# Attention and top-1 experts: q, k and v laid out in tiles before the launch, the bias added on VectorE

## The chip, the cores and the metric

One core of a Trainium2 chip: TensorE (PE, with its weight loads as PEld), VectorE (DVE), ScalarE (ACT), GpSimd (POOL), SyncE (SP, which issues most DMAs). The metric is the device time of one launch in microseconds. What numpy does to the arrays before the launch is not part of it.

## The reference

Attention over 8 batches, 8 heads, 576 positions and 64 features, with a causal window of 128 and a bias that falls linearly with distance; then each of the 4608 tokens goes to the one expert (of 8) with the largest cosine to it.

```python
scores = scale * np.matmul(q, k.transpose(0, 1, 3, 2))
rel = pos[:, None] - pos[None, :]
bias = slopes[:, None, None] * (-np.abs(rel).astype(np.float32))[None, :, :]
mask = (rel >= 0) & (rel < window)
scores = np.where(mask, scores + bias[None], -1000000000.0)
attn = np.exp(scores - np.max(scores, axis=-1, keepdims=True))
attn = attn / (np.sum(attn, axis=-1, keepdims=True) + 1e-09)
out = np.matmul(attn, v)
...
logits = xn @ en.T / tau              # xn, en: rows of x = attention's output and of expert_emb, normalized
expert_idx = np.argmax(logits, axis=1)
out[mask] = gate_w[mask, None] * (np.maximum(x[mask] @ w1[e], 0.0) @ w2[e])
```

## The kernel before, in words

The attention stage works on 36 tiles of 128 query rows, in the order of `tiles`: for each pair of batches, four tiles of the one (the first of kind "first", three "full"), four of the other, and a "pair" tile with the last 64 rows of both. Each tile is two units of four heads (72 units, `u`), so 16 first, 48 full and 8 pair units. A query sees its own tile's keys and the tile's before.

For each tile `load` (L413) brings q, k and v as 128 rows by 512 features, one piece of 64 floats per row and head. `prep_pe` (L492) turns q and k on TensorE (four matmuls each, against the identity, into a PSUM bank of tag "pt"), and `prep_copy` (L526 on VectorE, L528 on ScalarE) copies them to SBUF with features on the partitions, q with the factor -1/8. `on_dve` and `SHARE` deal out the copies between the two engines. A batch's keys lie in two blocks of SBUF, so that tile 2 of a batch takes its keys from both.

A unit then runs through these steps:
- `score_pe`: for each of two PSUM banks one bias matmul (L592; for a first tile the table `tab_first` against the identity, else the rank-two factors `row` and `col` that `factors` builds), then the products of q and k (L598) added onto it. The scores are negated, with the keys of the own tile and of the tile before side by side: 256 columns a head.
- `merge_dve` (L607, L610): one predicated copy takes, for each position in a window, the one of the two columns that is in it. First tiles need none.
- `max_dve` (L615): one reduction per bank, over the 128 columns of each of two heads.
- `exp_act` (L622) on ScalarE, one instruction for a head; `probs_pe` (L630) turns the probabilities on TensorE; `probs_act` (L481) and `probs_dve` (L484) write them as a high and a low half-precision part; `mask_pool` (L650, L663) on GpSimd separates what belongs to the own tile (`md`) from what belongs to the tile before (`mp`).
- `values_pe` (L682, L698): six matmuls a head, 24 a unit. In a pair tile the own part is three a head and the part before is three for each batch, whose operand has 64 rows of queries (36 a unit).
- `sums_dve` and `normalize` (L714, L720) divide by the sums.

After both units of a tile, x is split into two half-precision parts (`x_act` L734 and L736, `x_pool` L747), its norm is summed (L743), it is turned by a DMA (L751), and the logits are formed (L757, L761). Tiles are routed in groups of 8, 8, 8, 6, 4 and 2: a chain of small operations (L825 to L854) gives each token its place, and an indirect DMA from GpSimd (L863) puts its row into the expert's segment in DRAM.

Beside this the "head" runs: after the third group the expert with most tokens is picked, its weights are fetched and split (L912 on ScalarE, L916 on VectorE), and its first 384 rows are computed by TensorE (L945, L969) in whatever time is left. After the last put, the stage of the experts (`moe`) begins with L1374; it is not touched.

The order on each engine is not written by hand. `Plan` takes jobs with an engine, a duration in ns, what they follow, which buffers they make and use, and a due time (`STEP` times the unit plus `DUE` of the step); it lists them greedily, per engine the job that could start first, and among those within `SLACK` ns of it the one due first. Jobs with `fill=True` (the head's) come after all others. The queues then run in that order, each instruction waiting for its semaphores. Buffers: four PSUM banks for scores, two for turned probabilities and values (tag "ps"), two for turned q and k and small things (tag "pt").

## Time and profile before

| | |
|---|---|
| Median of three runs | 689.68 us (685.45 to 692.1) |
| The profiled execution | 690.15 us, its span 688.4 us, mean granted TensorE clock 0.971 |
| TensorE busy in the span | 643.3 us |
| VectorE, ScalarE, GpSimd busy | 377.8, 340.8, 261.4 us |

The span runs from the first to the last instruction of one execution. Rows of busy time count a stretch once however many instructions overlap in it. Instructions of one engine overlap: one that follows closely starts before the one in front has ended, so the pace of a kind is read from start to start, not from its duration. A half clock of TensorE (1.2 in place of 2.4 GHz) shows as 0.5 in the clock column.

### The profile page before, as it was taken

To read this page: it belongs to the slowest core of one execution; us is meant where nothing else is said; L and a number is where in the kernel's file an instruction comes from. 1 tells how busy PE (TensorE), PEld (TensorE's weight loads), DVE (VectorE), ACT (ScalarE), POOL (GpSimd) and SP (SyncE) were. 2 spreads that over 40 slices of the span, in tenths; PEclk is the share of its full clock that TensorE was granted. 3 is DMA by queue.
4 is the path that set the end of the run, shared out by engine and by line. 5 is a ranking of instruction groups with operands and counts; after the bars stand their busy time and mean duration, and the time that the engine had idled before them with its cause. 6 is when DMAs were issued, how large, how long until landed. Compare 5 with 4: busy or idle time off the path is not lost. (4 is left out here: it accounts for less than half of the span.)

```text
span 688.4 us, 15704 instructions
## 1 busy us (share of the span) xinstructions
PE 643.3 (93%) x6043; PEld 425.1 (62%) x6043; DVE 377.8 (55%) x974; ACT 340.8 (49%) x794; POOL 261.4 (38%) x472
## 2 busy tenths in 40 slices
PE   7999999999999988992999999999999999999993
PEld 4777767777776755641665467476584764754442
DVE  5877786776789969642335724344244255310250
ACT  5999888977887955410235523343243244210210
POOL 7667687767777837552010210120111112001011
PEclk9999999998999999886999999999999999999998
DMA  8588969886988895136999973934919545001000
GB/s 200 125 184 191 194 170 206 159 214 129 201 156 229 196 206 161 41 109 149 249 250 358 250 262 55 269 123 67 318 63 240 202 99 200 16 16 47 13 31 31
DMA packets 217676, 109.83 MB, mean 160 GB/s; under 512 B 195829, under 2 KB 195829, under 8 KB 217600
## 3 DMA queue, kind: packets, MB, share of 16 engines
q1 hardware_dynamic: 211760, 89.89, 55.7%
q0 software_dynamic: 5840, 18.92, 7.2%
q8 instruction: 48, 0.79, 0.5%
q14 instruction: 28, 0.23, 0.1%
HBM read 61.92 MB, written 28.12 MB: 131 GB/s over the span
## 5 line engine op out<-in xcount | busy, mean ns | idle before, releaser
L1374 PE MATMUL ps<-xT,w1h 128*128 128x272 f16 (+7 forms) x896 | 175.4, 296 | 13.4 <-DMA xT<-xs 12.2
L1374 PE MATMUL ps<-xT,w1l 128*128 128x272 f16 (+7 forms) x448 | 132.4, 296 | 0.0
L1374 PEld LDWEIGHTS <-w1h 128*128 128x128 f16 x896 | 88.2, 99 | 44.8 <-issue 14.1
L384 POOL DMA_INDIRECT out_dram<-y,ids x32 | 35.6, 1112 | 203.5 <-DVE y L1432 105.3
L1382 DVE SCALAR_TENSOR_TENSOR hl<-ps,hh 128x272 f16<-128x272 f32 (+7 forms) x112 | 51.7, 475 | 105.9 <-ACT hh L1384 99.5
L1384 ACT ACTIVATE hh<-ps 128x272 f16<-128x272 f32 (+7 forms) x112 | 45.6, 425 | 114.7 <-PE ps L1374 114.7
L622 ACT ACTIVATE pe<-sc,nm 128x128 f32<-128x128 f32 x288 | 87.7, 390 | 24.6 <-DVE nm L615 13.7
L1418 PE MATMUL ps<-w2h,hh 128*128 128x512 f16 (+1 forms) x264 | 98.4, 373 | 0.0
L1418 PE MATMUL ps<-w2l,hh 128*128 128x512 f16 (+1 forms) x264 | 98.4, 373 | 0.0
L1418 PE MATMUL ps<-w2h,hl 128*128 128x512 f16 (+1 forms) x264 | 98.4, 373 | 0.0
L1418 PEld LDWEIGHTS <-hh 128*128 128x128 f16 x528 | 51.5, 98 | 58.6 <-issue 0.8
L598 PE MATMUL sc<-k,q 64*128 64x128 f32 (+2 forms) x768 | 74.8, 339 | 0.5 <-ACT q L528 0.5
L484 DVE SCALAR_TENSOR_TENSOR pq<-ptp,pq 128x512 f16<-128x512 f32 x72 | 53.1, 738 | 20.3 <-ACT pq L481 18.1
L598 PEld LDWEIGHTS sc<-k,q 64*128 64x128 f32 (+1 forms) x768 | 51.0, 180 | 19.3 <-issue 16.4
L481 ACT ACTIVATE pq<-ptp 128x512 f16<-128x512 f32 x72 | 55.0, 764 | 14.4 <-PE ptp L630 8.8
L615 DVE TENSOR_REDUCE nm<-sc 128x2 f32<-128x256 f32 x144 | 58.5, 416 | 3.2 <-PE sc L598 2.9
L630 PE MATMUL ptp<-ident,pe 128*128 128x128 f32 x288 | 48.0, 287 | 8.0 <-ACT pe L622 3.6
L1349 DVE SCALAR_TENSOR_TENSOR w2l<-ws,w2h 128x1024 f16<-128x1024 f32 x28 | 33.9, 1223 | 36.2 <-ACT w2h L1351 36.0
L1374 PEld LDWEIGHTS <-w1l 128*128 128x128 f16 x448 | 44.1, 99 | 15.1 <-DVE w1l L1349 0.3
L1349 DVE SCALAR_TENSOR_TENSOR w1l<-ws,w1h 128x1024 f16<-128x1024 f32 x28 | 33.4, 1222 | 34.0 <-ACT w1h L1351 33.9
L747 POOL TENSOR_TENSOR gx<-xf,gx 128x512 f16<-128x512 f32 x36 | 42.7, 1187 | 19.7 <-ACT gx L734 8.5
L698 PE MATMUL av<-vh,mp 128*128 128x65 f16 (+1 forms) x512 | 49.0, 200 | 0.5 <-POOL mp L650 0.5
(233 smaller groups left out, 1174.1 us busy)
## 6 DMA issues: line engine op xcount, KB each, us to landing
ws<-moe_w_dram SPq DMA_DIRECT2D x56, 512.0 KB
ldk<-k_dram SPq DMA_DIRECT2D x32, 256.0 KB
ldq<-q_dram SPq DMA_DIRECT2D x32, 256.0 KB
ldv<-v_dram SPq DMA_DIRECT2D x32, 256.0 KB
stg<-moe_w_dram SPq DMA_DIRECT2D x16, 256.0 KB
xs<-zrow SPq DMA_DIRECT2D x3, 1092.2 KB
xs<-zrow SPq DMA_DIRECT2D x1, 1413.5 KB
xs<-zrow SPq DMA_DIRECT2D x1, 1285.0 KB
```

The costliest lines, as they stand in the source:

```text
L481: nc.scalar.activation(hi, ps, AF.Copy, scale=scale)
L484: nc.vector.scalar_tensor_tensor(lo, ps, scale, hi, op0=ALU.mult, op1=ALU.subtract)
L598: nc.tensor.matmul(sc[T, hf, j][o, l, w], qx[rows, hp, o], at["x"][rows, hp, kc], start=False, stop=(l == 1), skip_group_check=True)
L615: nc.vector.tensor_reduce(nm_t[T, hf][:, j, :], sc[T, hf, j][:, :, 0:P], axis=AX.X, op=ALU.min)
L622: nc.scalar.activation(pr_t[T, hf][:, 2 * l + j, :], ps[:, l, 0:P], AF.Exp, bias=nm[:, l : l + 1], scale=-1.0)
L630: nc.tensor.transpose(pt[:, i, :], pe[:, i, :], ident)
L698: nc.tensor.matmul(o_, a_, b_, start=False, stop=(n == last), skip_group_check=True)
L1349: nc.vector.scalar_tensor_tensor(lo_, x, SW, hi, op0=ALU.mult, op1=ALU.subtract)
L1374: nc.tensor.matmul(ps[:, :w], a[:, kt, fs], xx[:, b + kt, c0 : c0 + w], start=(n == 0), stop=(n == len(jobs) - 1))
L1382: nc.vector.scalar_tensor_tensor(hl[:, ft, c0 : c0 + w], ps[:, :w], 0.0, hi, op0=ALU.max, op1=ALU.subtract)
L1384: nc.scalar.activation(hi, ps[:, :w], AF.Relu)
L1418: nc.tensor.matmul(ps, x[:, ft, a * P : (a + 1) * P], w[:, ft, c], start=(n == 0), stop=(n == len(jobs) - 1))
```

## The change

Numpy now lays q out as one array per tile with 128 features (two heads) on the partitions, k as one per batch in blocks of 64 positions, also with features on the partitions, and v as one per tile with rows on the partitions. A tile's loads go straight into the operands of the score matmuls, with 2 KB in one piece for each partition, and a batch's keys lie in one SBUF tile. Turns, copies, the bias matmuls and their factors are gone; the factor 1/8 goes to the exponential. Two PSUM banks that they used become one, and turned probabilities and values get three. VectorE adds the bias from a table of 16-bit values and takes the maximum in one instruction for a head, after the merge, writing the sum back to PSUM: four in a unit in place of two reductions. For pair tiles `mask_pool` writes two operands of 128 rows, padded with zeros, so that all of their value matmuls are wide. The planner's jobs, prices, due times, step and slacks change with it. One cast of x in four goes to VectorE up to tile 26, as before, and none after (before: one in two).

```diff
-RING = {'sc':'sc','pt':'pt','ptp':'ps','av':'ps','lg':'pt','misc':'pt'}
-BANKS = {'sc':4,'ps':2,'pt':2}
+RING = {'sc':'sc','ptp':'ps','av':'ps','lg':'pt','misc':'pt'}
+BANKS = {'sc':4,'ps':3,'pt':1}
-KBUFS = {"k0": 2, "k1": 2, "q": 3}
+KBUFS = {"k": 3, "q": 4}
-STEP = 3038
-SLACK = {'PE': 100, 'ACT': 100, 'DVE': 50, 'POOL': 400, 'SP': 300}
+STEP = 2426
+SLACK = {'PE': 104, 'ACT': 98, 'DVE': 44, 'POOL': 541, 'SP': 49}
-SHARE = {'v': 0, 'x': 0.25, 'q': 0, 'k': 0, 'v2': 0, 'x2': 0.5, 'q2': 0.5, 'k2': 0.25}
+SHARE = {'v': 0, 'x': 0.25, 'v2': 0, 'x2': 0}
...
+    def bias_table(kind):
+        rel = rels[kind]
+        m = const.tile([P, P], I32, name=f"mask_{kind}")
+        wrap = const.tile([P, P], F32, tag="wrap", name=f"wrap_{kind}")
+        nc.vector.tensor_scalar(m, rel, 0.0, None, op0=ALU.is_ge)
+        nc.vector.tensor_scalar(wrap, rel, 0.0, float(WIN), op0=ALU.is_lt, op1=ALU.mult)
+        nc.vector.tensor_tensor(wrap, wrap, rel, op=ALU.add)
+        tab = const.tile([P, H, P], BF16, name=f"tab_{kind}")
+        for h in range(H):
+            nc.vector.tensor_scalar(tab[:, h, :], wrap, -slopes[h] / QS, None, op0=ALU.mult)
...
+        def load(T, nm):
+            kind, b, t = tiles[T]
+            if nm == "q":
+                qT[T] = qk.tile([P, HP, P], F32, tag="q", name=f"q_{T}", bufs=KBUFS["q"])
+                nc.sync.dma_start(qT[T], q[T].rearrange("p (a c) -> p a c", a=HP))
+            elif nm == "k":
+                for x in (b, b + 1) if kind == "pair" else (b,):
+                    if x not in kT:
+                        kT[x] = qk.tile([P, S // REM, HP, REM], F32, tag="k", name=f"k_{x}", bufs=KBUFS["k"])
+                    c = slice(P // REM * t, S // REM if kind == "pair" else P // REM * (t + 1))
+                    nc.sync.dma_start(kT[x][:, c], k[x].rearrange("p (n a c) -> p n a c", a=HP, c=REM)[:, c])
...
         def score_pe(T, hf):
...
-                nc.tensor.matmul(ps[:, :, 0 : b_.shape[-1]], a_, b_, start=True, stop=False, skip_group_check=True)
...
                         nc.tensor.matmul(
-                            sc[T, hf, j][o, l, w], qx[rows, hp, o], at["x"][rows, hp, kc], start=False, stop=(l == 1), skip_group_check=True
+                            sc[T, hf, j][o, l, w].rearrange("p (n c) -> p n c", c=REM),
+                            qT[T][rows, hp, o],
+                            kT[x][rows, kc, hp, :],
...
-        def max_dve(T, hf, j):
+        def max_dve(T, hf, j, l):
...
-            nc.vector.tensor_reduce(nm_t[T, hf][:, j, :], sc[T, hf, j][:, :, 0:P], axis=AX.X, op=ALU.min)
+            o_ = sc[T, hf, j][:, l, 0:P]
+            nc.vector.tensor_tensor_reduce(
+                o_, o_, tabs[tiles[T][0]][:, 4 * hf + 2 * l + j, :], -QS, BIG, ALU.add, ALU.min, nm_t[T, hf][:, j, l : l + 1]
+            )
...
                     if kind == "pair":
                         for a in range(2):
-                            o = slice(a * REM, (a + 1) * REM)
-                            jobs.append((n + 3, a, px[o, i, 0:w], mp[:, i, o, c], vS[pv_[a]][vi][:, h, :]))
+                            jobs.append((n + 3, a, px[:, i, 0:w], mp[a][:, i, :, c], vS[pv_[a]][vi][:, h, :]))
...
-                    f"score{u}", "PE", 750 if first else 1150 if pair else 1250, lambda a=a: score_pe(*a), makes=[(RING["sc"], x) for x in keys],
+                    f"score{u}", "PE", 530 if first else 900 if pair else 1080, lambda a=a: score_pe(*a), makes=[(RING["sc"], x) for x in keys],
...
-                    J(
-                        f"max{n}", "DVE", 335, lambda c=c: max_dve(*c), after=[f"merge{n}"] + ([f"max{u}_0"] if j else []),
+                    for l in range(2):
+                        J(
+                            f"max{n}_{l}", "DVE", 245, lambda c=c, l=l: max_dve(*c, l),
```

## Rows read from the trace of the kernel before

**Rows 1.** The page's first part: busy time of each engine over the whole span, with its share of the span and its number of instructions.
```profile
PE 643.3 (93%) x6043; PEld 425.1 (62%) x6043; DVE 377.8 (55%) x974; ACT 340.8 (49%) x794; POOL 261.4 (38%) x472
```

**Rows 2.** Busy time by stretch. Columns: the stretch in us from the span's start, its length, then busy us (and instructions) of PE, PEld, DVE, ACT and POOL, the granted TensorE clock (1.00 is full), the DMA engines' mean busy share, GB/s.
```profile
7.00:140.00 133.00, 126.30 (x1789) 97.17 (x1787) 101.36 (x307) 115.90 (x312) 97.30 (x177) 1.00 0.85 181
140.00:232.00 92.00, 87.58 (x1219) 67.55 (x1219) 75.81 (x240) 74.12 (x199) 67.25 (x122) 0.96 0.85 189
8.00:293.00 285.00, 266.43 (x3600) 200.35 (x3601) 224.00 (x676) 225.12 (x600) 198.46 (x349) 0.97 0.79 174
293.00:322.00 29.00, 17.32 (x97) 7.67 (x95) 10.97 (x57) 1.61 (x7) 12.05 (x27) 0.79 0.46 131
322.00:688.00 366.00, 354.05 (x2328) 214.53 (x2328) 138.54 (x218) 111.65 (x185) 46.11 (x79) 0.98 0.52 150
```

**Rows 3.** Instructions in order of time, the last normalization of the attention stage on DVE and the first expert matmul on PE. Columns: start us, duration us, engine, line, operation, written tile <- read tiles, shapes, count; in brackets the idle time before it and what ended it.
```profile
292.00 0.42 DVE L720 TENSOR_TENSOR xf<-av,rs 128x256 f32<-128x256 f32 x1
...
322.56 0.64 PE L1374 MATMUL ps<-xT,w1h 128*128 128x288 f16 x2 [12.24 <-DMA xT<-xs]
```

**Rows 4.** Who waited for whom, PE alone, 20 to 292 us, the two longest sums: us in total, times, longest us.
```profile
PE ps_head L945 <- DMA x_head<-xs: 2.6, 1, 2.6
PE ptp L630 <- ACT pe L622: 2.1, 3, 0.8
```

**Rows 5.** Instructions in order of time on PE around 62 us, in the steady attention stage (columns as in rows 3): a turn, a pair tile's bias and scores, and the values of a full tile up to the turn of probabilities after them.
```profile
61.72 0.60 PE L492 MATMUL ptq<-ident,ldq 128*128 128x128 f32 x4
62.25 0.33 PE L592 MATMUL sc<-col,row_pair 2*128 2x384 bf16 x2
62.52 0.88 PE L598 MATMUL sc<-k,q 64*64 64x192 f32 x16
63.33 0.17 PE L682 MATMUL av<-eone,erow 3*128 3x4 bf16 x1
...
64.17 0.63 PE L630 MATMUL ptp<-ident,pe 128*128 128x128 f32 x4
```

**Rows 6.** The same on PE between 12 and 22 us: bias and scores of a full tile with keys in one block, then the scores of one with keys in two blocks; the row after each shows where it ends.
```profile
12.23 0.39 PE L592 MATMUL sc<-col,row_full 2*128 2x512 bf16 x2
12.55 1.13 PE L598 MATMUL sc<-k,q 64*128 64x256 f32 x8
13.61 0.66 PE L492 MATMUL ptk<-ident,ldk 128*128 128x128 f32 x4
...
20.43 1.16 PE L598 MATMUL sc<-k,q 64*128 64x128 f32 x16
21.52 0.66 PE L492 MATMUL ptk<-ident,ldk 128*128 128x128 f32 x4
```

**Rows 7.** The same on PE around 134 us: the first matmul of a pair tile's values and the first instruction after them.
```profile
133.61 0.17 PE L682 MATMUL av<-eone,erow 3*128 3x4 bf16 x1
...
135.38 0.66 PE L492 MATMUL ptk<-ident,ldk 128*128 128x128 f32 x4
```

**Rows 8.** ScalarE. First two groups of instructions by line, 0 to 293 us (columns: line, engine, operation, tiles, shapes, count | busy us, mean ns | idle before, releasers), then two rows in order of time around 62 us, a read of an accumulator and what starts after it.
```profile
L528 ACT ACTIVATE k<-ptk 128x512 f32<-128x512 f32 (+1 forms) x36 | 20.4, 579 | 7.7 <-PE ptk L492 7.7
L528 ACT ACTIVATE q<-ptq 128x512 f32<-128x512 f32 x31 | 18.9, 608 | 0.5 <-PE ptq L492 0.5
...
62.08 0.23 ACT L743 ACTIVATION_READ_ACCUMULATOR junk<-xf 128x1 f32 x1
62.17 0.78 ACT L481 ACTIVATE pq<-ptp 128x512 f16<-128x512 f32 x1
```

**Rows 9.** Instructions in order of time on DVE around 62 us: two predicated copies of 128 elements, two reductions over 256, a fused multiply and subtract over 512, and what starts after it.
```profile
61.89 0.49 DVE L610 COPY_PREDICATED sc<-mask_pair,sc 128x128 f32<-128x128 int32 x2
62.29 0.76 DVE L615 TENSOR_REDUCE nm<-sc 128x2 f32<-128x256 f32 x2
62.98 0.75 DVE L484 SCALAR_TENSOR_TENSOR pq<-ptp,pq 128x512 f16<-128x512 f32 x1
63.62 0.49 DVE L610 COPY_PREDICATED sc<-mask_pair,sc 128x128 f32<-128x128 int32 x2
```

**Rows 10.** Groups of instructions by line on DVE, 0 to 293 us (columns as in rows 8).
```profile
L736 DVE CAST gx<-xf 128x512 f16<-128x512 f32 x11 | 7.0, 639 | 0.1
L916 DVE SCALAR_TENSOR_TENSOR w1l<-stg,w1h 128x512 f16<-128x512 f32 x8 | 6.6, 828 | 0.0
L916 DVE SCALAR_TENSOR_TENSOR w2l<-stg,w2h 128x512 f16<-128x512 f32 x8 | 5.9, 742 | 0.0
...
L526 DVE TENSOR_SCALAR q<-ptq 128x512 f32<-128x512 f32 x5 | 3.4, 686 | 0.0
L526 DVE TENSOR_SCALAR k<-ptk 128x512 f32<-128x512 f32 (+1 forms) x4 | 2.1, 554 | 1.1 <-PE ptk L492 1.1
```

**Rows 11.** Instructions in order of time at the start: the first scores on PE and the first reductions on DVE.
```profile
7.97 0.71 PE L598 MATMUL sc<-k,q 64*128 64x128 f32 x8 [0.52 <-ACT q L528]
...
10.32 0.75 DVE L615 TENSOR_REDUCE nm<-sc 128x2 f32<-128x256 f32 x2
```

**Rows 12.** Busy time and granted clock in three short stretches (columns as in rows 2).
```profile
154.00:156.00 2.00, 0.45 (x3) 0.14 (x1) 1.71 (x6) 1.49 (x5) 2.00 (x3) 1.00 0.53 208
156.00:160.00 4.00, 3.97 (x26) 2.41 (x27) 3.15 (x8) 2.61 (x7) 3.71 (x7) 0.54 0.94 126
...
232.00:234.00 2.00, 1.49 (x18) 1.03 (x17) 2.00 (x7) 1.91 (x5) 2.00 (x3) 1.00 1.01 239
```

More of the change, by code (lines that the diff above doesn't have):

```diff
@@ L401, in attention @@
         hp_ = actx.enter_context(tc.tile_pool(name="head", bufs=1))
-        loaded = {}
-        def load(T, which="qkv"):
+        loaded, qT, kT = {}, {}, {}
+        def load(T, nm):
             kind, b, t = tiles[T]
-            r = loaded.setdefault(T, {})
-            for nm, src in (("k", k), ("q", q), ("v", v)):
-                if nm not in which:
-                    continue
-                x = ld.tile([P, H, D], F32, tag=f"ld{nm}", name=f"ld{nm}_{T}")
-                if kind != "pair":
-                    nc.sync.dma_start(x, src[b, :, t * P : (t + 1) * P, :].rearrange("h p d -> p h d"))
-                else:
-                    for i in range(2):
-                        nc.sync.dma_start(
-                            x[i * REM : (i + 1) * REM], src[b + i, :, NF * P : S, :].rearrange("h p d -> p h d")
-                        )
-                r[nm] = x
-        load(0, "kq")
-        load(1, "kq")
+            if nm == "q":
[7 more added lines that the diff above has]
+                    nc.sync.dma_start(kT[x][:, c], k[x].rearrange("p (n a c) -> p n a c", a=HP, c=REM)[:, c])
+            else:
+                loaded[T] = x = ld.tile([P, H, D], F32, tag="ldv", name=f"ldv_{T}")
+                nc.sync.dma_start(x, v[T].rearrange("p (h d) -> p h d", h=H))
+        for T in range(2):
+            for nm in "kq":
+                load(T, nm)
         emb = const.tile([E, DM], F32, name="emb")
@@ L553, in v_lo @@
             vS[T][1] = lo
-            nc.gpsimd.tensor_tensor(lo, loaded[T]["v"], vS[T][0][:, :, 0:D], op=ALU.subtract)
+            nc.gpsimd.tensor_tensor(lo, loaded[T], vS[T][0][:, :, 0:D], op=ALU.subtract)
         tails = [keep.tile([P, 4, P, 2], F16, name=f"tails_{i}") for i in range(2)]
@@ L1003, in k_tiles @@
             return [T] + ([] if pv_ is None else list(pv_) if isinstance(pv_, tuple) else [pv_])
-        for n in "kq":
-            for T in range(2):
-                J(f"load_{n}{T}", "SP", 1456, lambda: None, makes=[("ld" + n, ("ld" + n, T))], due=-1e6 + T)
+        for T in range(2):
+            for n in "kq":
+                J(
+                    f"load_{n}{T}", "SP", 1100, lambda: None, due=-1e6 + T, uses=[(n, tiles[T][1] if n == "k" else T)],
+                    makes=[(n, (n, tiles[T][1] if n == "k" else T))] if n == "q" or not T else [],
+                )
         J("tables", "POOL", 2500, misc_tables, due=2000)
         J("expert_rows", "DVE", 300, expert_rows, after=["tables"], due=5000)
-        J("factors", "DVE", 3600, factors, due=STEP * 1.6)
         J("tails", "POOL", 900, lambda: [nc.gpsimd.memset(x, 0.0) for x in tails], due=STEP * 4, early=EXPERT)
         J("rel_pair", "POOL", 600, lambda: bias_rel("pair"), due=STEP * 4, early=EXPERT)
-        J("tab_pair", "DVE", 300, lambda: merge_mask("pair"), after=["rel_pair"], due=STEP * 6)
+        J("tab_pair", "DVE", 1500, lambda: bias_table("pair"), after=["rel_pair"], due=STEP * 6)
         last = None
```

198 lines of the change are left out of this document (64 added, 134 removed).

## The prediction, made before the changed kernel ran

> **What bounds the kernel now.** I read the page's first lines, then a table of busy times by stretch, then who waited for whom on TensorE, and only then instructions in order of time. The page gives TensorE 93% of the span and no other engine more than 55% [rows 1]; that is an average over two stages, so I split it. The attention stage runs to about 293 us, the experts from 322.6 us on [rows 2, 3]. In the first, from 8 to 293 us, TensorE is busy 266 of 285 us, VectorE 224, ScalarE 225, GpSimd 198 [rows 2]. A busy TensorE need not be the bound, so I looked for its waits: between 20 and 292 us the longest sum for one releaser is 2.6 us [rows 4]. It is never short of work for long, and no input load appears among its releasers. So the bound of this stage is the length of TensorE's queue; the other three have 60 to 87 us of slack. The expert stage is bounded by TensorE too (354 of 366 us) [rows 2], and the change does not touch it: it can only come earlier.
>
> Between the two lies a tail. The last normalization on VectorE starts at 292.00 and the first expert matmul at 322.56 [rows 3]. In those 30 us the last tiles are split, turned, routed, scattered and read back, one step after another, while TensorE is busy for 17 us with what is left of the head expert [rows 2]. I keep the 30 us: the change adds and removes nothing there. So the time gained is the time by which the last normalization comes earlier.
>
> **Part 1, what leaves TensorE.** Durations overlap on the engines, so I take start to start. A turn of one k or q tile (four matmuls) goes from 61.72 to 62.25, 0.53 us; there are 72: 38.2 us. The pair of bias matmuls takes 0.27 us in a pair tile (62.25 to 62.52) [rows 5] and 0.32 in a full one (12.23 to 12.55) [rows 6]; with 0.31 for a first tile, an estimate between these, 48 x 0.32 + 16 x 0.31 + 8 x 0.27 = 22.5 us. Scores with 256 columns go in 1.06 us (12.55 to 13.61); where a tile's keys lie in two blocks it is 16 shorter ones in 1.09 [rows 6]. Now every full tile has the first form: 16 x 0.03 = 0.5 us. A pair tile's values take 1.77 us (133.61 to 135.38) [rows 7], because 24 of its 36 matmuls write only 64 partitions; a full tile's 24 take 0.84 with their first one (63.33 to 64.17) [rows 5]. With all 36 wide and 0.11 for the first: 0.11 + 36 x 0.030 = 1.21, 8 x 0.56 = 4.5 us. Together 65.7 us, so TensorE would need 266.4 - 65.7 = 201 us. The strided key operand is costed at nothing: its blocks are 64 fp32 long; bounds -2 and +5 us over 56 units, and TensorE's new slack covers it.
>
> **Part 2, ScalarE and GpSimd.** ScalarE loses 67 copies, 20.4 + 18.9 = 39 us of busy time [rows 8], and takes over five casts for about 3: 225 becomes 189. GpSimd loses the small fills of the bias factors and gains selects and fills in eight pair units, for which the planner allows 1.6 us instead of 1.4: about 199 [rows 2]. Neither becomes the bound.
>
> **Part 3, what VectorE gains.** Before, one reduction covers two heads: two go from 62.29 to 62.98, 0.345 us each, and 144 cost 49.7 us. After, one fused add and minimum covers one head, 128 elements, and 288 are needed. No row of before shows this operation. From below: a predicated copy of 128 elements in PSUM takes 0.20 us (two go from 61.89 to 62.29) [rows 9]. From above: the same with a separate read of an accumulator, which on ScalarE takes 0.09 us (62.08 to 62.17) [rows 8]: 0.29. The planner of the changed kernel prices it at 245 ns, and its other VectorE prices stand near the rows (335 for the reduction that shows 345, 202 for the copy that shows 200), so I take 0.245: 70.6 us, that is +20.9. Off VectorE go its share of the copies, 3.4 + 2.1 = 5.5 us, and five of eleven casts, 7.0 x 5/11 = 3.2 [rows 10]. The tables for pair tiles replace the factors: nothing net, bounds -2 and +2. VectorE: 224 + 20.9 - 5.5 - 3.2 = 236 us.
>
> Here a page of the Trainium skill speaks against the change. VectorE: DVE Perf Modes, section Two Vector instructions with no wait between them, says that an operation which writes out its accumulator is really two instructions, the main one and a read. On VectorE no row of before shows this; on ScalarE the trace agrees, with the 0.09 us above. By that rule, with ScalarE's price, the sum is the first rival below; without it, at 0.20 us, VectorE would need 13 us less than I take.
>
> **The sum.** The most loaded engine is now VectorE, 236 us, ahead of TensorE at 201. Before, the bound engine was busy for 126.3 of 133 us and then 87.6 of 92, 95% [rows 2]; I give VectorE 95.5%: 236 / 0.955 = 247 us. It begins at about 8 us: the first scores start at 7.97 and the first reduction at 10.32 [rows 11]; without turn and copy the first scores can come a little sooner. At the end the chain of the last unit leaves VectorE idle for about 5 us, an estimate: twice the 2.35 us between the first scores and the first reduction [rows 11], since exponentials, turning, masks and values still follow the last maximum; I take this as filled by the low parts of the head's weights, 6.6 + 5.9 = 12.5 us of work [rows 10] that may run when nothing else is ready. So the last normalization is at 8 + 247 = 255 us in place of 292: 37.5 us sooner. The profiled execution took 690.15 us, 0.5 above the median of 689.68; 690.15 - 37.5 = 652.6, against the median about 652.5.
>
> The loads cost nothing. They are off every chain now [rows 4], and fewer and longer pieces can only help. On SP, a k or q load now waits until an earlier tile's scores have read its buffer, where it waited for a turn; behind it stand the transposing loads of x and the head's weights, which TensorE and VectorE need later. With four q buffers that wait is over before the tile is wanted; if not, I allow 4 us. The longer queue of scores has no fewer buffers than before: scores keep four banks, and turned probabilities and values get three for two.
>
> **Rivals.** First, the fused operation costs 0.29 us because its accumulator is read out separately: 288 x 0.045 = 13 us more, 666. For it stands the row on ScalarE, against it the planner's price. Second, the half clock comes oftener. In the rows TensorE's clock falls to 0.54 of full (1.2 GHz in place of 2.4) after a stretch in which it was busy only 0.45 of 2 us; while it was busy 1.49 of 2 us the clock stayed at 1.0 [rows 12]. At 201 of 247 us it would be 81% busy, nearer to the second. If four more stretches of 7 us were at the half clock, TensorE would fall behind by 14 us, of which its slack gives most back: I price it at 10, 663. Third, the low parts of the head's weights are starved while VectorE is full, and the whole head expert, which took TensorE's fill time until now, lands in the 30 us tail. It needs about 31 us at full clock (8 x 12 x 0.162 and 72 x 0.216 from the planner's prices, which is an estimate) and starts some us after its weights: the experts start 7 us late, 660. Fourth, on the other side: the fused operation streams its data once for each of its two operations, 2 x 0.20 = 0.40 us. Then VectorE has 45 us more, 47 at its share, and the time is 700, slower. It decides from 0.37 us on: (0.37 - 0.245) x 288 / 0.955 is 37.5. Against it: the fused multiply and subtract over 512 elements goes from 62.98 to 63.62 [rows 9], 0.64 us, 3.2 times the copy of 128 and so a single pass, and the planner's price is far from it. Fifth, the change does not do what it says: the pace of a unit is set by the chain through the four score banks. A unit holds two of them for about 1.06 + 1.6 + 0.5 us of work and 0.6 of handing on, 3.8 us (the rows for scores and maxima, the planner's prices for the rest), so two units in flight allow one each 1.9 us, while VectorE needs 3.3. That speaks against it; it would leave 688.
>
> **How the numbers follow.** Forecast 0.56, first rival 0.18, second 0.09, third 0.10, fourth 0.04, fifth 0.03. A change below 1%, about 7 us, can't be told from none here. Faster by over 1%: 0.93; within 1%: 0.03; slower: 0.04. The low end: 0.20 us for the fused operation, 13 us, and 97% busy, 4 more: 635. The high end takes the first rival with the third or with a busy share of 93%: 674.
>
> **What would show it.** Right: no turn and no bias matmul in the trace, scores of 256 columns at 1.06 us, the fused operation at 0.245 us start to start, VectorE busy in 95% or more of 20 to 240 us and TensorE in some 80%, waits of TensorE on ScalarE and VectorE in place of none, the last normalization near 255 us, and 30 us from there to the first expert matmul. Wrong: a fused operation at 0.29 or over, a clock below 0.9 in the attention stage, VectorE with more than 10% of idle time, which would say that buffers or the order of the queue set the pace, or a tail longer than 34 us.

## The result, and the profile after

| | before | changed |
|---|---|---|
| median of the runs, us | 690.89 (685.45 to 692.87) | 669.12 (664.06 to 670.26) |
| profiled execution, us (span) | 690.15 (688.4) | 670.26 (668.1) |
| last normalization starts, us | 292.00 | 266.81 |
| first expert matmul starts, us | 322.56 | 300.57 |

The ratio is 0.971 (95% interval 0.965 to 0.976): faster by 2.9%, where 5.4% was forecast. A second measurement of the same kernel beside other runs of the kernel before gave 666.89 us and 0.963 (0.961 to 0.966). So the time lies inside the range, toward the high end, and the gain is somewhat over half of the forecast.

The page's first part for the changed kernel, against [rows 1]:

```profile
PE 603.2 (90%) x5483; PEld 391.7 (59%) x5483; DVE 396.4 (59%) x1385; ACT 313.1 (47%) x732; POOL 258.2 (39%) x487
```

TensorE still leads over the whole span. The table by stretch shows that this is now the expert stage alone (columns as in [rows 2]):

```profile
8.00:267.20 259.20, 216.82 (x2964) 160.58 (x2965) 238.98 (x1071) 193.39 (x529) 196.46 (x350) 0.89 0.75 192
267.20:300.60 33.40, 27.24 (x168) 14.18 (x167) 15.72 (x74) 6.58 (x17) 12.35 (x27) 0.97 0.43 117
300.60:668.00 367.40, 354.10 (x2328) 214.62 (x2328) 138.34 (x218) 111.31 (x185) 44.61 (x79) 0.98 0.53 150
```

Up to the last normalization VectorE (third of the busy columns) has 239.0 of 259.2 us, 92%, and TensorE 216.8, 84%; before it was 224 and 266 of 285 [rows 2]. The bound of this stage has changed engines, as forecast. The three rows also give the sizes: the attention stage lost 25.2 us, the tail after it grew from 30.6 [rows 3] to 33.8, the expert stage from 365.9 to 367.5. -25.2 + 3.2 + 1.7 = -20.3, the difference of the spans.

The two instructions that mark the stages, as in [rows 3]:

```profile
266.81 0.43 DVE L653 TENSOR_TENSOR xf<-av,rs 128x256 f32<-128x256 f32 x1
...
300.57 0.64 PE L1300 MATMUL ps<-xT,w1h 128*128 128x288 f16 x2 [6.16 <-DMA xT<-xs]
```

TensorE now waits, where it did not before [rows 4]. The three longest sums of who waited for whom between 8 and 267 us (columns as in [rows 4], which has PE alone):

```profile
PEld ptp L561 <- ACT pe L553: 39.8, 55, 3.5
ACT pe L553 <- DVE nm L544: 32.1, 30, 3.8
PE ptp L561 <- ACT pe L553: 17.5, 31, 2.2
```

Its transposes wait for the exponentials (17.5 us of PE alone, where it was 2.1), and these for the negated maxima of VectorE: the wait is passed up to VectorE. VectorE's own waits in this stretch are short; the two longest sums:

```profile
DVE sc L535 <- PE sc L521: 5.6, 8, 1.4
DVE pq L468 <- ACT pq L465: 3.2, 5, 0.8
```

The new operation, in order of time on VectorE around 60 us:

```profile
59.94 0.30 DVE L544 CUSTOM_DVE_ANT_0 sc<-sc,tab_first 128x128 f32<-128x128 f32 x1
60.16 0.14 DVE L544 DVE_READ_ACCUMULATOR2_ANT nm<- 128x1 f32 x1
60.16 0.33 DVE L544 CUSTOM_DVE_ANT_0 sc<-sc,tab_first 128x128 f32<-128x128 f32 x1
60.40 0.14 DVE L544 DVE_READ_ACCUMULATOR2_ANT nm<- 128x1 f32 x1
60.40 0.17 DVE L703 COPY gl<-ptl 128x16 f32<-128x16 f32 x1
60.49 0.29 DVE L544 CUSTOM_DVE_ANT_0 sc<-sc,tab_first 128x128 f32<-128x128 f32 x1
```

It is two instructions, and the second costs nothing: whatever follows starts at the same time as the read of the accumulator (60.16 and 60.16, 60.40 and 60.40). Start to start the pair takes 0.22 to 0.24 us here; from the start of the operation to the start of its read it is 0.221 us on average over all 288.

### The profile page after: what moved, and what is told of

It is laid out like the page before. It is cut to its first block, busy times and chain, and to the rows that moved or that the text cites. A ratio compares the mean times of both kernels' runs of the same rounds, so it can differ in the third digit from the quotient of the medians.

```text
span 668.1 us, 14943 instructions
## 1 busy us (share of the span) xinstructions
PE 603.2 (90%) x5483; PEld 391.7 (59%) x5483; DVE 396.4 (59%) x1385; ACT 313.1 (47%) x732; POOL 258.2 (39%) x487
## 5 line engine op out<-in xcount | busy, mean ns | idle before, releaser
L553 ACT ACTIVATE pe<-sc,nm 128x128 f32<-128x128 f32 x288 | 86.3, 375 | 47.7 <-DVE nm L544 37.6
L561 PE MATMUL ptp<-ident,pe 128*128 128x128 f32 x288 | 59.0, 317 | 33.4 <-ACT pe L553 17.5
L521 PE MATMUL sc<-k,q 64*128 64x256 f32 (+2 forms) x640 | 82.7, 409 | 0.0
L561 PEld LDWEIGHTS ptp<-ident,pe 128*128 128x128 f32 x288 | 35.8, 154 | 50.3 <-ACT pe L553 39.8
L1275 DVE SCALAR_TENSOR_TENSOR w2l<-ws,w2h 128x1024 f16<-128x1024 f32 x28 | 33.9, 1223 | 37.5 <-ACT w2h L1277 37.5
L1275 DVE SCALAR_TENSOR_TENSOR w1l<-ws,w1h 128x1024 f16<-128x1024 f32 x28 | 33.4, 1221 | 36.4 <-ACT w1h L1277 36.3
L631 PE MATMUL av<-vh,mp 128*128 128x65 f16 x512 | 51.5, 199 | 3.1 <-POOL mp L581 1.4
L544 DVE CUSTOM_DVE_ANT_0 sc<-sc,tab_full 128x128 f32<-128x128 f32 x192 | 54.2, 306 | 0.3
```

The costliest lines, as they stand in the source:

```text
L521: nc.tensor.matmul(sc[T, hf, j][o, l, w].rearrange("p (n c) -> p n c", c=REM), qT[T][rows, hp, o], kT[x][rows, kc, hp, :], start=True, sto ...
L544: nc.vector.tensor_tensor_reduce(o_, o_, tabs[tiles[T][0]][:, 4 * hf + 2 * l + j, :], -QS, BIG, ALU.add, ALU.min, nm_t[T, hf][:, j, l : l + 1]
L553: nc.scalar.activation(pr_t[T, hf][:, 2 * l + j, :], ps[:, l, 0:P], AF.Exp, bias=nm[:, l : l + 1], scale=-1.0)
L561: nc.tensor.transpose(pt[:, i, :], pe[:, i, :], ident)
L631: nc.tensor.matmul(o_, a_, b_, start=False, stop=(n == last), skip_group_check=True)
L1275: nc.vector.scalar_tensor_tensor(lo_, x, SW, hi, op0=ALU.mult, op1=ALU.subtract)
```

## The experiments

In the table, "VectorE" is its busy time from 8 us to the start of the last normalization (a row of the table by stretch for each kernel, ended 0.4 us after that start), "idle" the rest of that stretch. The ratio is to the kernel before in the same set of runs. That kernel took 691 us in the first set (e2 to e5), 678 in the second (e1, e6 to e8), 692 in the third, 689 in the fourth (e10, e11), on different chips. The changed kernel itself ran in neither the second nor the fourth set, so there the stage times are compared, not the medians. On the chip of the second set the kernel before was 2% faster, and what the changed kernel would take there is not known (at its ratio of 0.971 it would be 658 us): a difference of a few us between it and e1, e6, e7 or e8 is not shown by this table. The expert stage took 365 to 370 us in all runs.

In e2, e9, e11 and a0 the instructions of VectorE up to the last normalization run in the very order of the changed kernel. In the others the queues were planned anew, with the prices or terms changed, and a new order is part of what they show.

| run | us | ratio | last normalization | VectorE | idle |
|---|---|---|---|---|---|
| changed | 669.1 | 0.971 | 266.8 | 239.0 | 20.2 |
| a0 the same again | 666.9 | 0.963 | 263.9 | 238.3 | 18.1 |
| e1 merges twice | 703.4 | 1.036 | 303.1 | 273.7 | 21.9 |
| e2 TensorE kept busy | 667.5 | 0.965 | 266.7 | 238.7 | 20.4 |
| e3 old order | 681.6 | 0.987 | 283.6 | 236.7 | 39.3 |
| e4 layout undone | 686.1 | 0.993 | 285.2 | 235.3 | 42.3 |
| e5 bias undone | 688.5 | 0.996 | 291.9 | 255.6 | 28.7 |
| e6 VectorE lighter | 664.5 | 0.979 | 262.4 | 225.9 | 28.9 |
| e7 head's weights first | 670.7 | 0.988 | 275.8 | 243.0 | 25.2 |
| e8 v's low part twice | 693.1 | 1.022 | 295.5 | 249.7 | 38.3 |
| e9 v's low part left out | 654.2 | 0.947 | 250.2 | 224.2 | 18.4 |
| e10 casts to ScalarE | 664.1 | 0.963 | 262.8 | 227.9 | 27.4 |
| e11 as e8, order held | 683.0 | 0.988 | 282.2 | 245.8 | 28.9 |

**Is VectorE the bound (e1)?**

```diff
-                nc.vector.copy_predicated(ps[:, :, 0:P], m, ps[:, :, P : 2 * P])
+                for _ in range(2):
+                    nc.vector.copy_predicated(ps[:, :, 0:P], m, ps[:, :, P : 2 * P])
...
-                        f"merge{n}", "DVE", 0 if first else 202 if pair else 335, lambda c=c: merge_dve(*c),
+                        f"merge{n}", "DVE", 0 if first else 404 if pair else 670, lambda c=c: merge_dve(*c),
```

> Every merge of the windows on VectorE is issued twice (the second writes the same values again), with its price in the order doubled: 56 + 56 full ones of 0.335 us and 16 of 0.2 us, about 37 us more on VectorE and nothing else. Theory (VectorE bounds the attention stage, 20 of 259 us idle): the 37 us come out in full or nearly, 28 to 37 us longer: 697 to 706. Rival (the chain over ScalarE and TensorE, or TensorE itself, ends last and VectorE is only well filled): its 20 idle us take up half, 15 to 20 us: 684 to 689.

Measured: the last normalization at 303.1, 36.3 us later than in the changed kernel. (The expectation counted 112 full copies; it is 96, 96 x 0.335 + 16 x 0.2 = 35.4.) The row by stretch, to set beside the changed kernel's:

```profile
8.00:303.50 295.50, 230.80 (x2967) 169.69 (x2968) 273.65 (x1194) 200.78 (x531) 198.12 (x350) 0.86 0.62 168
```

VectorE's busy time went up by 34.7 us and its idle time did not shrink (21.9 us, in the changed kernel 20.2): what VectorE has more to do comes out at the end. The rival, in which the idle time takes half of it, falls. That 34.7 meets the 35.4 of the sum is luck, though. Two copies onto the same bank take longer than twice one of 0.335 us:

```profile
61.72 0.88 DVE L536 COPY_PREDICATED sc<-mask_full,sc 128x256 f32<-128x256 int32 x2
62.51 0.74 DVE L468 SCALAR_TENSOR_TENSOR pq<-ptp,pq 128x512 f16<-128x512 f32 x1
```

From 61.72 to 62.51 it is 0.79 us, and 0.46 us from the first copy to the second at the median, so the copies added some 45 us. The operations that lie wholly in SBUF took 11 us less than in the changed kernel (36.9 against 48.0 us); what they depend on is the matter of e8 and e9.

**Is it TensorE's clock (e2)?**

```diff
             pt = bank("ptp", [P, 4, P], name=f"ptp_{T}_{hf}")
+            for _ in range(2):
+                nc.tensor.matmul(pt, ones, ones.unsqueeze(1).to_broadcast([P, 4, P]), start=True, stop=True)
             for i in range(4):
```

> Two extra matmuls of 128x512 go into the probabilities' bank ahead of the four transposes of each half tile, 72 x 2, where TensorE now waits for the exponentials (PEld ptp <- ACT pe 37.6 to 39.8 us in the changed kernel); nothing they write is read. Theory (VectorE sets the pace of the attention stage, 93% busy from 8 to 260 us): the clock's half-speed stretches of that stage, eleven with some 51 us, become fewer, and the time stays within 1% of the changed kernel's 669, because TensorE is not what ends last; TensorE's 31 us more of work fit into 42 us of its idle time only in part, so up to 5 us longer. Rival (the half clock is what the forecast lacks): the half-speed stretches go and the time falls by about 10 us, to 659. Second rival (TensorE bounds the stage): plus 20 us or more, 690.

```profile
8.00:267.10 259.10, 230.16 (x3107) 166.12 (x3107) 238.73 (x1071) 193.80 (x528) 197.12 (x350) 0.94 0.73 190
```

The granted clock of the stage rose from 0.89 to 0.94, TensorE's busy time from 216.8 to 230.2, and the last normalization came at 266.7 in place of 266.8. So the half-clock stretches are real, but the end is not set by them, and TensorE had room for 144 more matmuls. (The run changes the clock and TensorE's work together; what it shows is that both together leave the end where it was.) Ratio 0.965 (0.960 to 0.970): no change that can be told.

**What is the order worth (e3)?** The changed kernel with `STEP`, `SLACK` and `DUE` of the kernel before:

```diff
-STEP = 2426
-SLACK = {'PE': 104, 'ACT': 98, 'DVE': 44, 'POOL': 541, 'SP': 49}
+STEP = 3038
+SLACK = {'PE': 100, 'ACT': 100, 'DVE': 50, 'POOL': 400, 'SP': 300}
...
```

> The changed kernel with the step, the slacks and the due times of the kernel before (the layout and the bias part stay changed). Theory: the work of VectorE is the same, so the stage's need stays 239 us; an order made for a slower stage leaves VectorE more idle time than the 20 us of now: 675 to 685. Rival (the new order is a by-product and costs or gives nothing): 669 within 3. Second rival (the new order itself costs, since it lets TensorE's clock fall): 655 to 664.

```profile
8.00:284.00 276.00, 230.02 (x3026) 167.24 (x3025) 236.73 (x1094) 197.14 (x537) 199.69 (x350) 0.89 0.67 180
```

VectorE's busy time is no longer (236.7 us), but 39.3 us are idle in place of 20.2, and the last normalization comes 16.8 us later. Some of that is won back: more of the head's work is done by then, and the tail is 29.2 us in place of 33.8. The time, 681.6, is where the theory put it. Against this one other order, more than half of the gain, 12.5 of 22 us, hangs on the new one, which the prediction had taken for granted.

**One part at a time (e4, e5).** In e4 q and k are loaded as they lie in memory, turned by TensorE and copied by ScalarE, with the banks and buffers of before and due times for the turns; v stays laid out and the bias stays on VectorE.

```diff
-BANKS = {'sc':4,'ps':3,'pt':1}
...
+BANKS = {'sc':4,'ps':2,'pt':2}
...
+                nc.tensor.matmul(
+                    pt[:, hp, :], x[:, hp * P : (hp + 1) * P], ident, start=(hp == 0), stop=(hp == HP - 1),
...
+                nc.scalar.activation(qT[T], pt, AF.Copy)
```

> The layout part undone: q and k come in as they lie in memory, TensorE turns them (72 turns of 0.5 us, 37 us) and ScalarE copies them (39 us), with two banks for the turns and two for probabilities and values as before; bias and maximum stay on VectorE; k keeps 2 buffers and q 3. Theory (VectorE bounds the changed kernel, TensorE the one before): TensorE's need in the attention stage goes from 210 to 247 us and passes VectorE's 239, so the last normalization comes 10 to 25 us later: 680 to 694. Rival (TensorE bounds already): the full 37 us, 706. Second rival (the layout part was worth nothing, all gain came from the bias): 669 within 3.

```profile
8.00:285.60 277.60, 240.58 (x3288) 184.87 (x3289) 235.31 (x1089) 229.47 (x639) 197.73 (x350) 0.94 0.77 179
```

686.1 us, inside the theory's 680 to 694. But no engine is at its limit: TensorE 240.6 of 277.6 us (87%), VectorE 235.3, ScalarE 229.5. So the theory's number came true without its mechanism being shown; the due times were made for a kernel without these turns, and e3 shows what that alone can cost. In e5 the bias goes back to TensorE's matmuls and VectorE takes plain maxima:

```diff
+                nc.tensor.matmul(ps[:, :, 0 : b_.shape[-1]], a_, b_, start=True, stop=False, skip_group_check=True)
...
-            nc.vector.tensor_tensor_reduce(
-                o_, o_, tabs[tiles[T][0]][:, 4 * hf + 2 * l + j, :], -QS, BIG, ALU.add, ALU.min, nm_t[T, hf][:, j, l : l + 1]
-            )
+            nc.vector.tensor_reduce(mx_t[T, hf][:, j, :], sc[T, hf, j][:, :, 0:P], axis=AX.X, op=ALU.max)
...
+            nc.vector.tensor_scalar(nm_t[T, hf][:, j, :], mx_t[T, hf][:, j, :], -QS, None, op0=ALU.mult)
```

> The bias part undone: the bias is added by a matmul of two rows ahead of the scores on TensorE (0.31 us for a half tile, 72 of them, 22 us), and VectorE takes one plain maximum for two heads (0.345 us, 144 of them) and a small negation (0.08 us); the layout stays changed. Theory (VectorE bounds): VectorE's sum is 144 x 0.425 = 61 us in place of 288 x 0.22 = 63 us, so the same need, TensorE 232 of 252 us: 669 to 678. Rival (TensorE bounds): plus 22 us, 691. Second rival (the fused operation on VectorE costs more than the trace shows, by contention): 655 to 664.

688.5 us: the theory's 669 to 678 was missed, and the rival's 691 was met for a reason that it does not name. The groups by line on VectorE up to 292 us:

```profile
L569 DVE TENSOR_REDUCE mx<-sc 128x2 f32<-128x256 f32 x144 | 59.6, 414 | 0.0
L572 DVE TENSOR_SCALAR nm<-mx 128x2 f32<-128x2 f32 x144 | 57.0, 396 | 0.9
```

The negation of two numbers per partition, priced at 0.08 us, took 396 ns on average: 57 us of VectorE, which therefore needed 255.6 us. The kernel before has no such step (it takes a minimum of scores with the sign turned), so e5 is no clean undoing of the bias part and its worth stays unpriced. It shows something else, in order of time:

```profile
59.91 0.15 DVE L572 TENSOR_SCALAR nm<-mx 128x2 f32<-128x2 f32 x1
...
60.85 0.64 POOL L607 TENSOR_SCALAR_AFFINE_SELECT md<-pq 128x512 f32<-128x512 f32 x1 [1.46 <-DVE pq L485]
...
61.44 0.64 POOL L607 TENSOR_SCALAR_AFFINE_SELECT mp<-pq 128x512 f32<-128x512 f32 x1
61.75 0.35 DVE L572 TENSOR_SCALAR nm<-mx 128x2 f32<-128x2 f32 x1
...
62.04 1.16 POOL L706 TENSOR_TENSOR gx<-xf,gx 128x512 f16<-128x512 f32 x1
62.34 0.17 DVE L673 RECIPROCAL rs<-av 128x4 f32<-128x4 f32 x1
62.46 0.85 DVE L572 TENSOR_SCALAR nm<-mx 128x2 f32<-128x2 f32 x1
```

At 59.91 GpSimd is idle and the negation takes 0.15 us. At 61.75 it ends at 62.10, with GpSimd's select (61.44 + 0.64 = 62.08); at 62.46 it ends at 63.31, just behind GpSimd's subtraction (62.04 + 1.16 = 63.20). The reciprocal of 62.34, whose input lies in PSUM, is not held. So the tiny operation in SBUF waited for the end of what GpSimd was doing. Over all 144 negations it is the same: 75 took more than 0.25 us, all of them begun while GpSimd was at work, and 74 of these ended within 0.15 us behind the end of one of its instructions; of the 31 begun while GpSimd was idle none took that long.

**Does GpSimd slow VectorE (e8, e9, e11)?** In e8 the subtraction that makes v's low part is issued twice and its price doubled:

```diff
-            nc.gpsimd.tensor_tensor(lo, loaded[T], vS[T][0][:, :, 0:D], op=ALU.subtract)
+            for _ in range(2):
+                nc.gpsimd.tensor_tensor(lo, loaded[T], vS[T][0][:, :, 0:D], op=ALU.subtract)
...
-                f"v_lo{T}", "POOL", 1113, lambda T=T: v_lo(T), after=[f"v_hi{T}"],
+                f"v_lo{T}", "POOL", 2226, lambda T=T: v_lo(T), after=[f"v_hi{T}"],
```

> The subtraction that makes the low part of v on GpSimd is issued twice (the second writes the same values), 36 x 1.1 = 40 us more on GpSimd (193 to 233 of 252 us busy), nothing more on VectorE, with its price in the order doubled. Theory (VectorE's small operations and casts are stretched while GpSimd runs, which is what makes its sum 239 us where the forecast had 222 for the same operations at their shortest): VectorE's busy time from 8 to 267 us grows by 3 to 8 us, and the end comes as much later: 672 to 677. Rival (the stretch has nothing to do with GpSimd): VectorE's busy time stays, 669 within 2. Second rival (GpSimd with 233 us is itself the next bound, by the wait of the values on its masks): more than 10 us, 680 or more.

```profile
8.00:295.90 287.90, 231.13 (x3008) 167.41 (x3008) 249.65 (x1082) 196.65 (x534) 238.38 (x386) 0.89 0.68 172
```

(The 222 us in the expectation are not the forecast's; that was 236.) VectorE's busy time grew by 10.7 us, its idle time by 18, and the last normalization came 28.7 us later: more than theory and first rival allow, and with GpSimd at 238 of 288 us not plainly the second rival either. The order had changed with the price, so the opposite was tried with the order held: no subtraction at all. A tile of zeros, filled once, stands in for v's low part, so e9 leaves out a part of the computation; TensorE still multiplies by it.

```diff
-            nc.gpsimd.tensor_tensor(lo, loaded[T], vS[T][0][:, :, 0:D], op=ALU.subtract)
...
+            vS[T][1] = loaded["vz"]
```

> Left out: the low part of v, which is zero here; TensorE still multiplies by it. GpSimd loses 36 subtractions of 1.12 us, 40 of its 206 us between 8 and 267 us; the prices in the order stay, so the order of every queue stays that of the changed kernel. Theory (VectorE bounds and GpSimd is only near; the doubling cost 28 us because it made GpSimd the bound): VectorE still needs its 239 us, so the last normalization can come at most 12 us earlier, and 4 to 8 us are expected: 661 to 665 beside a changed kernel of 669. Rival (VectorE's casts and small operations are stretched by GpSimd's work): VectorE's busy time to the last normalization falls by 4 to 9 us as well, and the last normalization comes 10 to 17 us earlier: 652 to 659. Second rival (GpSimd bounds the stage): 20 us earlier or more, 649 or less. Third (GpSimd does not matter from below): within 2 of the changed kernel.

It ran beside a0, the changed kernel again:

> The changed kernel once more, unaltered. The last four experiments ran beside a kernel before of 678.0 us, the four ahead of them beside one of 691.1, so the changed kernel is wanted beside the same runs as those that follow. Theory (the ratio is the kernel's): 0.971 of the kernel before, whatever that takes here: 671 beside 691, 658 beside 678. Rival (the changed kernel's time is its own, 669, and only the kernel before varies from chip to chip): 0.987 beside 678.

a0 gave 0.963 of the kernel before, on its 692 us: both readings of its expectation predict nearly the same there, so they are not told apart. The rows by stretch, a0 first:

```profile
8.00:264.40 256.40, 218.63 (x2966) 161.94 (x2967) 238.29 (x1082) 193.85 (x531) 197.36 (x350) 0.87 0.76 192
```

```profile
8.00:250.60 242.60, 206.59 (x2970) 153.88 (x2967) 224.19 (x1082) 193.25 (x530) 158.34 (x315) 0.94 0.79 203
```

GpSimd lost 39 us, and VectorE, with the same 1082 instructions, lost 14.1 us of busy time. Its idle time did not change (18.1 and 18.4), and the last normalization came 13.8 us earlier. This is the first rival: the end lies in its range, and VectorE's busy time fell by even more than its 4 to 9 us. TensorE's clock rose too, from 0.87 to 0.94, but in e2, where it rose as far, the end did not move. Which instructions were freed is seen in the groups by line on VectorE, a0 first:

```profile
L544 DVE CUSTOM_DVE_ANT_0 sc<-sc,tab_full 128x128 f32<-128x128 f32 x192 | 54.0, 305 | 0.3
L468 DVE SCALAR_TENSOR_TENSOR pq<-ptp,pq 128x512 f16<-128x512 f32 x72 | 52.7, 732 | 3.5 <-ACT pq L465 3.3
...
L669 DVE CAST gx<-xf 128x512 f16<-128x512 f32 x6 | 4.9, 814 | 0.1
...
L778 DVE TENSOR_TENSOR lg<-lg,oh 128x64 f32<-128x64 f32 (+1 forms) x4 | 2.8, 709 | 0.0
L763 DVE TENSOR_TENSOR rz<-rz,ry 128x8 f32<-128x8 f32 (+1 forms) x4 | 2.5, 636 | 0.0
```

```profile
L545 DVE CUSTOM_DVE_ANT_0 sc<-sc,tab_full 128x128 f32<-128x128 f32 x192 | 53.8, 302 | 0.3
L468 DVE SCALAR_TENSOR_TENSOR pq<-ptp,pq 128x512 f16<-128x512 f32 x72 | 52.6, 730 | 4.2 <-ACT pq L465 4.1
...
L670 DVE CAST gx<-xf 128x512 f16<-128x512 f32 x6 | 3.6, 603 | 0.1
...
L764 DVE TENSOR_TENSOR rz<-rz,ry 128x8 f32<-128x8 f32 (+1 forms) x4 | 0.9, 232 | 0.0
...
L779 DVE TENSOR_TENSOR lg<-lg,oh 128x64 f32<-128x64 f32 (+1 forms) x4 | 0.9, 224 | 0.0
```

What touches PSUM keeps its duration (305 and 302, 732 and 730 ns); the casts and the operations of two inputs that lie wholly in SBUF fall to three quarters or a third. Summed over all VectorE instructions of the stretch, those with a tile in PSUM (and the accumulator reads) take 191.9 us in a0 and 192.5 in e9, the 137 others 46.3 and 31.7: all of the difference is in these 137. Not every one of them is held: the 15 reciprocals (0.18 us) and the 23 reductions (0.21 us) among them took the same on average in both. The Trainium skill has a rule for this: SBUF — State Buffer, section Terms, says that VectorE and GpSimd share a pair of SBUF ports, given out as an exclusive lock for a whole instruction, so that the loser waits in full. The rows of e5, where VectorE's operation ends 0.02 and 0.11 us behind GpSimd's, and the 14.1 us of e9 agree with it.

Last, the doubled subtraction with the order held (the price stays 1113):

> The low part of v is again made twice on GpSimd, 40 us more there, but the price in the order stays at one, so that every queue has the order of the changed kernel. Theory (each us of GpSimd's subtraction costs VectorE 0.35 us, 14 us for 40 as its removal gave back, and GpSimd itself, with 237 us and its waits, ends up beside VectorE): VectorE's busy time to the last normalization grows by 10 to 14 us, the last normalization comes 14 to 25 us later: 682 to 693. Rival (the 28 us of the first doubling came from GpSimd as the bound, and VectorE is not slowed by more than 5): 690 to 700 with VectorE's idle time above 40 us. Second rival (the first doubling lost by its other order): 669 to 676.

```profile
8.00:282.60 274.60, 219.17 (x2965) 164.15 (x2966) 245.75 (x1081) 195.73 (x530) 236.90 (x386) 0.89 0.71 180
```

The end is as the theory has it (15.4 us later than the changed kernel, 18.3 later than a0, 683 us), VectorE's part of it is not: 7 us more, not 10 to 14. Its SBUF operations take 53.1 us (a0: 46.3), the others 192.7: it is again the former that grew, though not in proportion. The rest, 9 to 11 us, is new idle time. e8 has the same instructions in another order, and its last normalization comes 13 us later; but more of the head's work is done by then, and over the whole span it is 8 us (690.3 against 682.5), on different chips.

**Can VectorE be relieved (e6, e10), and the tail shortened (e7)?** e6 gives ScalarE the remaining casts, the copies of the logits and the normalization of every third tile; e10 gives it the casts and copies only.

```diff
-SHARE = {'v': 0, 'x': 0.25, 'v2': 0, 'x2': 0}
+SHARE = {'v': 0, 'x': 0, 'v2': 0, 'x2': 0, 'n': 0.34}
...
-            nc.vector.tensor_copy(gl[gi][:, g, :], lgs.pop(T))
+            nc.scalar.activation(gl[gi][:, g, :], lgs.pop(T), AF.Copy)
```

> Work of VectorE goes to ScalarE: all casts of the attention output (9 more), the copies of the logits (36), and the normalization of every third tile (24 half tiles, each as four scaled copies of 128x64). VectorE loses about 9 x 0.6 + 36 x 0.09 + 24 x 0.42 = 19 us, ScalarE gains some 28 (190 of 252 us busy before it). Theory (VectorE bounds): the last normalization comes 12 to 19 us earlier, 650 to 657. Rival (a second limit is close behind: ScalarE with 218 us and the chain from scores to transposes through it): a gain of 0 to 8 us, 661 to 669. Second rival (ScalarE's queue delays the exponentials, and with them TensorE): slower, 670 to 680.

> Only the light half of the move that took work from VectorE: the remaining casts of the attention output (6 in the attention stage, 0.8 to 0.9 us each) and the copies of the logits (36 of 0.17 us) go to ScalarE, no normalization does. VectorE loses 11 us, ScalarE gains 9 (193 to 202 of 257 us). Theory (VectorE's row bounds the stage with an idle time of about 20 us that stays, and the heavier move lost part of its gain because ScalarE's 219 us delayed the exponentials): the last normalization comes 8 to 11 us earlier: 656 to 660 beside a changed kernel of 667 to 669, 0.95 of the kernel before. Rival (any other order of the queues loses what it gains, as the one with the head's splits ahead did): 664 to 672.

VectorE is busy 13 us less in e6 and 11 less in e10, as meant, but 7 to 9 us of it came back as idle time, and the last normalization came only 4.4 and 4.0 us earlier (1.2 in e10 against a0):

```profile
8.00:262.80 254.80, 210.33 (x2989) 155.07 (x2990) 225.89 (x1018) 219.24 (x669) 196.82 (x350) 0.96 0.76 195
```

```profile
8.00:263.20 255.20, 212.79 (x2994) 157.76 (x2991) 227.85 (x1048) 201.89 (x574) 197.60 (x350) 0.93 0.78 195
```

e10 at 0.963 (0.959 to 0.967) can't be told from the changed kernel; the rival was right. ScalarE's load does not explain it, since with 219 us in e6 and 202 in e10 the idle time is nearly the same (28.9 and 27.4); a different order is left as the reason, argued and not shown. For e6 even the sign is open: its 664.5 us are 0.979 of the kernel before, where the changed kernel has 0.971 and 0.963. In e7 the splits of the head's weights no longer count as fill work:

```diff
...
-            J(f"wlo{i}", "DVE", 850, lambda i=i: part_lo(i), after=[f"whi{i}"], uses=[("stg", i)], due=d + 5500, fill=True)
+            J(f"wlo{i}", "DVE", 850, lambda i=i: part_lo(i), after=[f"whi{i}"], uses=[("stg", i)], due=d + 5500)
```

> The splits of the head's weights (24 casts on ScalarE, 24 subtractions on VectorE) are no longer fill work that any attention work goes ahead of; they go by their due time. Theory (the tail between the last normalization and the first expert matmul grew by 3.2 us because the head's last products and their VectorE steps stand among the route chain's): the head is done sooner, the tail falls back by 2 to 3 us, while the splits push VectorE's attention work back by as much or less: 664 to 670. Rival (the tail is a chain of its own that the head does not touch): 669 or, by the delayed attention work, up to 674.

```profile
8.00:276.20 268.20, 225.85 (x3046) 166.81 (x3046) 243.01 (x1084) 197.63 (x536) 196.91 (x350) 0.92 0.71 184
```

(The expectation counts 24 splits; the trace has 16 casts and 16 subtractions.) The tail fell from 33.8 to 28.0 us (first expert matmul at 303.75), and the last normalization came 9.0 us later. By then all 16 subtractions are done, and all 8 times that VectorE makes the low part of the head's hidden values (`hl_head`); in the changed kernel it is 11 and 2, in the kernel before 16 and 8. So the tail does depend on the head's work, and buying it back costs more. No version that keeps the computation is measurably faster than the changed kernel.

## Why the prediction was right, and where its size came from

The forecast for the profiled execution comes to a span of 650.9 us (688.4 less 37.5); it is 668.1, 17.2 more. By its own steps:

- **The bound moves from TensorE to VectorE: right, and shown.** What VectorE has more to do comes out at the end (e1), 14 us taken from it come back in full (e9), 144 more matmuls on TensorE cost nothing (e2). What the layout and the bias are worth each is not shown, since e4 and e5 change more than the one part.
- **The fused operation at 0.245 us: a little high.** It takes 0.221, 63.6 us for 288, 7 less than forecast. The first rival was right that the accumulator is read by an instruction of its own, as the prediction cites it from the Trainium skill (VectorE: DVE Perf Modes, section Two Vector instructions with no wait between them), and the trace agrees: 288 reads behind 288 operations. Its price of 0.045 us is wrong here, since the read overlaps the next instruction. The fourth rival (two passes) falls, and so does the fifth (the chain through the score banks sets the pace): the time did fall, and VectorE's row is the full one.
- **VectorE's need, 236 us: 239.0, near by luck, since errors nearly cancel.** Without the fused operation it is 239.0 - 63.6 = 175.4 in place of 165.4, although some 5 us of the head's work (5 subtractions and 6 low parts) that stood in the row of before now come after the last normalization. I had carried VectorE's other operations over at their durations of before. Those that lie in SBUF depend on what GpSimd does meanwhile: the casts, 639 ns before [rows 10], took 938 in the changed kernel. e9 shows that GpSimd's subtraction of v alone costs VectorE 14 of the 239 us. That GpSimd's work slows more of them now because it is packed into 259 us (196, 76%) and not 285 (198, 70%) is argued, not shown. Summed in the same way as for e9, the operations wholly in SBUF took 42.7 us before (145 of them), 48.0 in the changed kernel (135), but 38.2 in e3 (144) and 36.9 in e1 (139), with 196 to 200 us of GpSimd in each: their cost changes with the order, and is no price that can be carried over.
- **"I give VectorE 95.5%": the step that failed.** It had 92.2%, 20 us idle where I counted 11: 9 of the 17 us. The share was borrowed from TensorE, which had a long queue of work that waited for next to nothing (2.6 us [rows 4]); VectorE stands in the middle of the chain, and waits for scores, probabilities and values as the others wait for it. It is not the end of the stage: 13.9 of the 20.2 us lie between 20 and 240 us, where VectorE is busy 206.1 of 220 us, 93.7%, and the prediction's sign of being right asked for 95. The idle time is not the clock's (20.4 us in e2), and GpSimd with 39 us less to do does not shorten it (18.4 in e9); with another order it goes to 39 (e3). What the least possible would be was not tried, so how much of it the chain demands stays open.
- **The tail kept at 30 us: 33.8, 3.2 us of the miss.** This is the third rival in part: 5 of the head's 16 subtractions and 6 of its 8 low parts now lie behind the last normalization, beside the route chain, and the first expert matmul is 3 us late where that rival said 7. The prediction had let all of this work fill VectorE's idle time. e7 shows the connection.
- **The expert stage untouched: 1.7 us longer.** No run isolates this.
- **Second rival, the half clock: right in the trace, without effect on the end.** The clock of the stage fell from 0.97 to 0.89, below the 0.9 that the prediction names as a sign of being wrong, and TensorE was busy 216.8 us where the forecast had 201. In e2 the clock came back to 0.94, with 144 more matmuls, and the end did not move.
- **The new order, not priced at all.** The diff changes step, slacks and due times; I wrote as if any good order came with the work. By e3 it carries some 12 us of the gain against the old one.

Together: 3.0 (need) + 9.2 (idle time, with roundings) + 3.2 + 1.7, 17.1 of the 17.2.

## What to carry to other kernels

When a change moves the bound to another engine, do not give the new one the old one's busy share: look at who waits for whom around it, and price the queue order as a part of the change, because with the same work another order cost 12 us here (e3). Before counting an engine's work from its durations, ask which of its operations lie wholly in SBUF while GpSimd is working. To test a cost, change the work and hold the order: in the three runs that did so (e2, e9, e11) a difference can be put down to the edit, and in most of those that were planned anew (e6, e7, e8, e10) the order covered what was asked; in e1, the nearness of the sums was luck. And run the kernel that a test is compared with on the same chip: here the kernel before differed by 2% between chips.

## What the runs showed of the hardware that was not expected

- A multiplication of two numbers per partition on VectorE took 110 to 1880 ns (e5), by what GpSimd was doing; 40 us of GpSimd's subtractions cost VectorE 14 us (e9), 40 more of them only 7 (e11). VectorE's operations with a tile in PSUM changed by less than 1% in the sum (191.9 us in a0, 192.5 in e9, 192.7 in e11).
- The accumulator read behind the fused add and minimum shows 0.14 us of duration and costs none, start to start: what follows begins with it (60.16 and 60.16 us).
- TensorE's granted clock over the attention stage went from 0.97 to between 0.86 and 0.96 in these kernels; in e2, the run that tests it, this did not set the end.
